# Forgetting attention followed by a gated convolutional FFN on one core: a new order of work, ReLU and weight casts allowed on two engines, the forget gates in one transfer, the last chunk in halves

## The chip, the core and the metric

The kernel runs on one core of a Trainium2 chip. Five engines work side by side, each through its own queue, strictly in the order of that queue: TensorE (PE in the profile, with its weight loads as PEld), VectorE (DVE), ScalarE (ACT), GpSimd (POOL), and SyncE (SP), which does nothing here but issue transfers. An engine whose next instruction waits also holds back everything behind it. Matmuls write PSUM, which this kernel holds as four tiles of 1024 fp32 columns (`ps0` to `ps3`); ACT or DVE has to empty a tile before PE may fill it again. The metric is device microseconds of the whole run; lower is better.

## The reference

Per batch and head (8 x 8, 576 positions of 64 values), causal attention with a decay from the forget gates f, then, on the heads joined to 512 channels, a feed-forward block whose hidden value is gated by a three-tap convolution of itself.

```python
cum = np.cumsum(np.log(np.clip(f, 1e-4, 1.0)), axis=-1)
scores = q @ k.T / 8 + cum[:, :, :, None] - cum[:, :, None, :]   # causal
attn = softmax(scores);  x = (attn @ v) joined to (8, 576, 512)
h = np.maximum(x @ w_in, 0.0)                    # 512 -> 1024
conv = w0 * h[s-1] + w1 * h[s] + w2 * h[s+1]     # along the sequence, per channel
out = (h * sigmoid(conv)) @ w_out                # 1024 -> 512
```

## The kernel before, in words

The program is a list of named tasks (class `Plan`). `ORDER` is the sequence in which the tasks are recorded, and so the sequence in which each engine's queue is filled; `name@ENGINE` chooses the engine where a task may run on more than one. Tiles that are reused (PSUM, score buffers, output buffers) are handed out in that sequence too. Nothing is rescheduled afterwards.

Work goes by half batch (hb 0 to 15: four heads, one PSUM-sized group each) and by batch (b 0 to 7). For half batch `hb` with its two head pairs `i = 2hb` and `2hb+1`:

- `q{hb}.0`, `q{hb}.1`: SP brings q and k from memory with a transposing DMA (`load_qk`, L230), for hb 0 and 1 by plain loads `ld`, PE transposes `tp` and an adjusting copy `cl` (`turned_qk`). The result lies in one of four `qk` tiles (hb modulo 4).
- The decay enters the scores as two more rows of the contraction. hb 1 to 7 get them by `cl` (DVE, L236) and `rw` (L252, L253: rows from the DRAM tensor `image`), hb 8 to 15 by `fi` (`fill`, L244 blanks and L246 rows of `image`), which may go only when both transposes of its half batch have landed. `ki` (POOL) writes `image`; hb 0 adds the decay with extra matmuls.
- `sd`, `so`, `st`: scores on PE (diagonal, off-diagonal, last 64 rows). `ed`, `eo`, `et`: their exponentials on ACT (L401, L418, L380), out of PSUM. `md`, `mt`: causal masks on POOL for hb 8 and later.
- `v{b}.x`: loads of v; `va`: casts of v to fp16; `pv`: attn @ v on PE (L442, L446); `n`: division by the row sum on DVE (L454, L456); `t` and `tx`: transposes on PE and their copies, two of them by DMA (hb 14 and 15).

For batch `b` and hidden chunk `ff` (0 to 7): `f` is x @ w_in (8 matmuls, L482), `r` the ReLU out of PSUM into the fp16 tile `ht` (L492), `c` and `d` the convolution on DVE into `u` (L497, L499), `a` a tanh on ACT (L502), `g` the gate on DVE (L506). The sigmoid is written as half of 1 + tanh, so the ReLU carries a factor of 0.5. `o{b}.{c}` is the product with w_out for 128 rows (L517), `k` copies the last 64 rows aside so that two batches share one matmul group, `e` empties PSUM into an output buffer `ob` (three of them; L523, for the last batch L527), `s` stores it. The weights come by `wi` and `wo` into the same `ob` buffers, and `wic` and `woc` cast them to fp16 (L560).

At the start ACT's queue issues two loads of f (rows 0 to 63 and 64 to 127 of one tile, the same data), loads the table for the logarithm, issues the convolution weights, and takes the logarithm (`dcl`, L313), then loads the table for exp (L314); DVE clips (`dca`, L568), scans (`dcs`) and forms the decay rows (`dck`).

Of the kernel before, what the change touches and what calls it, by code (L numbers as in the profile page):

```python
# [22 lines left out]
n1.0 n1.1 so5.0 t1 q5.0 tx0@DVE eo5.0 tx1@ACT cl3.0 ed5 f0.0 cl5.0 so4.0 r0.0 st2 wi2 c0.0 d0.0 so4.1 f0.1 et2 eo4.1
r0.1 c0.1 d0.1 q5.1 f0.2 v1.0 v1.1 rw3 h0 wic3@POOL eo4.0 v1.4 v1.3 a0.0 wic2@POOL f0.3 r0.2 f0.4 so5.1 a0.1 cl5.1
g0.0 r0.4 c0.4 f0.5 v1.2 rw5 g0.1 r0.3 eo5.1 sd6 r0.5 f0.6 d0.4 a0.4 c0.3 wo2 so6.1 r0.6 q4.1 eo6.1 c0.5 c0.6 st3 et3
sd7 wo1 va2.0@DVE d0.6 so6.0 ed6 pv2.0 sd10 ed7 g0.4 n2.0 va2.1@DVE d0.5 q4.0 c0.2 wo0 va3.0@ACT q6.0 eo6.0 woc2@POOL
f0.7 r0.7 pv2.1 so7.0 v4.0 n2.1 so7.1 ed10 eo7.0 eo7.1 so10.1 d0.3 d0.2 va3.1@POOL cl4.1 st5 eo10.1 sd11 cl4.0 pv3.0
pv3.1 ed11 et5 so11.0 a0.5 a0.2 n3.0 n3.1 woc0@POOL t2 t3 a0.6 rw4 tx2@DVE tx3@DVE so11.1 so10.0 wo3 eo11.0 c0.7 d0.7
q6.1 a0.3 v2.0 v2.4 g0.3 eo10.0 v2.3 woc1@POOL eo11.1 g0.5 f1.0 r1.0 f1.1 f1.2 g0.6 g0.2 f1.3 f1.4 a0.7 v2.2 r1.2 v2.1
g0.7 r1.3 r1.1 c1.0 woc3@ACT c1.2 sd9 st4 va4.0@POOL et4 r1.4 sd8 ed8 d1.0 h1 so9.1 o0.0 ed9 so8.1 cl6.0 cl6.1 so9.0  # L30
o0.1 c1.3 c1.4 va4.1@POOL d1.3 a1.0 g1.0 eo9.1 d1.4 eo9.0 so8.0 f1.5 eo8.1 d1.2 eo8.0 r1.5 rw6 sd12 q7.1 st6 pv4.0
va5.0@POOL va5.1@ACT et6 q7.0 e0.0@DVE c1.1 pv4.1 n4.0 a1.2 k0@DVE a1.4 n4.1 g1.4 ed12 a1.3 q9.1 sd13 zc g1.3 f1.6
ed13 r1.6 t4 tx4@ACT cl7.0 so12.1 eo12.1 pv5.0 pv5.1 c1.6 f1.7 n5.0 n5.1 so12.0 g1.2 r1.7 cl7.1 eo12.0 d1.1 so13.1
c1.7 d1.6 v3.0 v3.4 so13.0 v3.3 rw7 t5 eo13.1 c1.5 d1.5 eo13.0 tx5@ACT v3.2 q9.0 o0.2 v3.1 a1.6 a1.1 o0.3 f2.0 g1.1
e0.1@ACT f2.1 r2.0 a1.5 r2.1 d1.7 c2.0 g1.6 f2.2 st7 v4.2 g1.5 c2.1 et7 a1.7 f2.3 r2.2 fi9 r2.3 sd15 ed15 so15.0 f2.4
eo15.0 d2.0 so15.1 h2 g1.7 sd14 eo15.1 a2.0 ed14 c2.2 d2.2 c2.3 r2.4 d2.1 va7.0@DVE o1.0 c2.4 so14.0 so14.1 eo14.0
eo14.1 va6.0@POOL va6.1@POOL pv6.0 sd18 o1.1 q8.1 ed18 k1@DVE f2.5 d2.4 sd19 a2.4 n6.0 so19.0 g2.4 va7.1@POOL s0.1
e1.0@ACT d2.3 r2.5 pv7.0 ed19 pv7.1 eo19.0 q8.0 st9 et9 v4.3 c2.5 v4.4 n7.0 n7.1 g2.0 v5.0 f2.6 v4.1 md18 a2.2 so19.1
a2.1 fi8 pv6.1 eo19.1 d2.5 f2.7 so18.0 q10.0 md19 r2.6 g2.1 n6.1 s1.0 g2.2 a2.5 r2.7 o1.2 eo18.0 a2.3 t6 c2.6 t7 c2.7
tx6@ACT va8.0@POOL so18.1 tx7@DVE o1.3 f3.0 d2.7 eo18.1 d2.6 f3.1 g2.3 a2.7 va8.1@POOL e1.1@ACT r3.0 sd17 so17.1 g2.5  # L40
g2.7 a2.6 g2.6 r3.1 ed17 c3.0 d3.0 q10.1 f3.2 r3.2 c3.1 f3.3 eo17.1 c3.2 va9.0@DVE r3.3 c3.3 mt9 md17 sd16 ed16 v5.2
o1.4 so16.0 h3 eo16.0 so17.0 d3.2 v5.4 d3.1 d3.3 e1.2@ACT o2.0 fi10 pv9.0 n9.0 k2@DVE st8 q11.0 eo17.0 a3.0 et8 o2.1
a3.1 g3.1 a3.2 sd21 f3.4 va9.1@DVE g3.2 v5.3 s1.2 q11.1 ed21 a3.3 r3.4 e2.0@ACT pv9.1 n9.1 c3.4 f3.5 f3.6 g3.0 r3.5
st10 mt8 d3.4 md16 r3.6 c3.6 so16.1 eo16.1 s1.1 f3.7 so21.0 md21 et10 mt10 sd20 d3.6 o2.2 v5.1 r3.7 eo21.0 c3.7 g3.3
o2.3 a3.4 fi11 q12.0 ed20 a3.6 pv8.0 q12.1 sd23 v6.0 c3.5 st11 e2.1@ACT md20 s2.1 d3.7 a3.7 et11 g3.4 n8.0 va10.0@POOL
pv8.1 n8.1 sd22 so20.0 ed23 d3.5 ed22 t8 tx8@DVE eo20.0 md22 t9 so20.1 tx9@DVE a3.5 va11.0@DVE q13.1 so22.0 eo20.1
g3.6 so22.1 eo22.0 fi12 f4.0 f4.1 r4.0 g3.7 c4.0 d4.0 eo22.1 g3.5 q13.0 mt11 f4.2 r4.1 f4.3 so23.0 so21.1 r4.2 h4
eo23.0 r4.3 a4.0 f4.4 c4.2 d4.2 r4.4 md23 so23.1 v6.2 eo21.1 c4.3 o3.0 o3.1 va10.1@POOL sd25 c4.1 d4.3 a4.2 eo23.1
e3.0@ACT sd24 pv10.0 d4.1 ed24 md24 ed25 fi13 so25.1 c4.4 va11.1@ACT d4.4 q14.1 g4.0 pv10.1 n10.0 a4.3 n10.1 eo25.1
pv11.0 g4.2 a4.1 st12 et12 f4.5 r4.5 mt12 pv11.1 g4.3 f4.6 st13 n11.0 sd26 n11.1 t10 a4.4 g4.4 r4.6 c4.6 et13 ed26  # L50
s3.0 so24.0 c4.5 d4.5 f4.7 d4.6 k3@DVE md25 q14.0 eo24.0 v6.4 o3.2 t11 s2.0 o3.3 tx10@ACT a4.5 r4.7 g4.5 v6.1 sd27
a4.6 c4.7 so26.0 tx11@ACT ed27 v6.3 g4.6 e3.1@ACT s3.1 md26 g4.1 v7.0 d4.7 f5.0 f5.1 r5.0 r5.1 so27.1 eo27.1 c5.0
eo26.0 f5.2 c5.1 d5.1 so25.0 eo25.0 mt13 r5.2 o3.4 md27 so24.1 e3.2@DVE c5.2 d5.2 a4.7 f5.3 va12.0@POOL eo24.1 d5.0
g4.7 r5.3 so26.1 eo26.1 c5.3 so27.0 h5 a5.1 f5.4 f5.5 g5.1 a5.0 va12.1@POOL g5.0 eo27.0 r5.5 d5.3 fi14 o4.0 r5.4 c5.5
sd29 ed29 pv12.0 d5.5 q15.1 n12.0 a5.3 f5.6 va13.0@ACT s3.2 c5.4 st14 v7.4 et14 g5.3 va13.1@DVE v7.1 a5.5 r5.6 o4.1
f5.7 sd28 e4.0@ACT md29 pv13.0 r5.7 c5.6 so28.0 q15.0 ed28 g5.5 v7.3 d5.6 eo28.0 pv12.1 o4.2 c5.7 d5.7 a5.6 n12.1 v7.2
t12 pv13.1 n13.0 d5.4 g5.6 a5.7 a5.2 k4@POOL so29.1 n13.1 g5.7 tx12@ACT o4.3 eo29.1 fi15 a5.4 e4.1@ACT va15.0@POOL t13
s4.1 tx13@DVE sd30 sd31 va14.0@DVE so30.0 f6.0 ed30 md28 va14.1@POOL so29.0 eo30.0 g5.2 r6.0 f6.1 f6.2 va15.1@POOL
eo29.0 c6.0 r6.1 ed31 f6.3 st15 g5.4 d6.0 h6 c6.1 md30 r6.2 r6.3 so28.1 so30.1 et15 c6.2 eo28.1 eo30.1 so31.1 s0.0
c6.3 f6.4 mt15 eo31.1 d6.3 d6.2 pv14.0 mt14 md31 r6.4 n14.0 a6.2 pv14.1 n14.1 k5@DVE g6.2 c6.4 so31.0 eo31.0 f6.5 f6.6  # L60
f6.7 a6.3 r6.6 a6.0 g6.3 c6.6 r6.7 d6.1 pv15.0 d6.6 pv15.1 n15.0 n15.1 a6.6 tx14 tx15 g6.0 a6.1 c6.7 r6.5 o5.0 o5.1
o5.2 c6.5 o5.3 d6.5 a6.5 d6.7 f7.0 f7.1 d6.4 e5.0@ACT g6.6 a6.7 g6.1 a6.4 g6.5 f7.2 g6.4 r7.0 c7.0 g6.7 r7.1 c7.1 f7.3
f7.4 r7.3 e5.1@ACT r7.2 d7.0 f7.5 h7 d7.1 a7.0 a7.1 r7.5 c7.2 o6.0 g7.0 o6.1 o7.0.0 r7.4 g7.1 d7.2 c7.4 o7.1.0 o7.2.0
k6@ACT c7.3 o7.0.1 o7.3.0 c7.5 s5.0 d7.3 o7.2.1 a7.2 g7.2 o7.1.1 d7.4 f7.6 k7.1@DVE e6.0@ACT r7.6 c7.6 o5.4 s6.0
e5.2@ACT o7.2.2 o7.0.2 s5.1 f7.7 a7.3 r7.7 d7.5 a7.5 g7.3 c7.7 o7.3.1 k7.2@DVE o7.3.2 o6.2 d7.7 s5.2 o7.2.3 o7.0.3
a7.4 o7.1.2 o6.3 a7.7 d7.6 g7.4 g7.5 o7.2.4 o7.2.5 o7.1.3 a7.6 o7.1.4 o7.1.5 g7.6 o7.0.4 g7.7 e6.1@ACT k7.3@ACT
k7.5@DVE o7.0.5 o7.0.6 o7.0.7 e7.0@ACT o7.1.6 k7.6@DVE s4.0 s6.1 k7.0@POOL o7.2.6 o7.2.7 k7.4@ACT o7.1.7 e7.1@DVE
# [40 lines left out]
def kernel(  # L108
# [164 lines left out]
    nc.scalar.dma_start(fsb[BH:128], f.rearrange("b h s -> (b h) s"))
# [217 lines left out]
    def relu(b, ff):  # L491
        nc.scalar.activation(ht_of(b, ff)[:, 1:1 + S], ps_of(f"f{b}.{ff}")[:, 0:S], AF.Relu, scale=0.5)  # L492
# [31 lines left out]

    def evac_chunk(b, c, e):
        o, i = ob_t[slot[f"e{b}.{c & ~1}", "ob"]][:, c % 2, :], ps_of(f"o{b}.{c & ~1}.0")[:, 512 * (c % 2):512 * (c % 2 + 1)]
        (nc.scalar.copy if e == "ACT" else nc.vector.tensor_copy)(o, i)  # L527
# [209 lines left out]
```

## Time and profile before

| | us |
|---|---|
| median of 3 runs (lowest, highest) | 255.62 (255.13, 256.41) |
| the profiled execution, whole | 255.41 |
| its span on the core | 253.6 |
| around the span | 1.8 |
| PE, DVE, ACT busy | 231.1, 213.5, 211.4 |
| POOL busy | 62.0 |

The profile is of one execution. Its rows give start and length of an instruction, the line of the kernel that issued it, the tiles that it writes and reads, and in square brackets how long the engine had been idle and which work ended the wait. A queue named SPq or ACTq shows that engine issuing a transfer. The chain that ended last is followed back from the last instruction, each step to what released it.

### The profile page before, as it was taken

The page shows a single profiled execution, that of the slowest core. Times are in us where ns is not written, and L with a number is a line of the kernel's source. Part 1 is how long each engine was busy: PE and PEld are TensorE (multiplying, and loading weights), DVE is VectorE, ACT ScalarE, POOL GpSimd, SP SyncE. Part 2 cuts the span into 40 slices and gives each one's busy share as a digit, 9 for nine tenths or more (in the row PEclk, how much of TensorE's full clock was granted, in tenths as well). Part 3 has the DMA queues.
Part 4 walks back from the last instruction along what each step waited for, and adds up shares of the span by engine and source line. Part 5 has one row for each costly group of instructions (what it writes and reads, how often), then busy time and mean ns, then how long its engine had stood idle before and what let it go on. Part 6 is the DMA issues. An engine that isn't in the chain of part 4 may idle for free.

```text
span 253.6 us, 6451 instructions
## 1 busy us (share of the span) xinstructions
PE 231.1 (91%) x2654; PEld 147.4 (58%) x2654; DVE 213.5 (84%) x329; ACT 211.4 (83%) x283; POOL 62.0 (24%) x91
## 2 busy tenths in 40 slices
...
GB/s 185 320 229 165 222 209 256 215 246 195 236 197 195 215 181 214 216 227 224 217 225 205 187 239 193 197 210 264 230 213 231 87 87 50 24 108 3 277 132 170
DMA packets 116278, 48.81 MB, mean 192 GB/s; under 512 B 106274, under 2 KB 106274, under 8 KB 116248
## 3 DMA queue, kind: packets, MB, share of 16 engines
...
q10 hardware_dynamic: 246, 0.44, 0.6%
...
## 4 chain that ended last, share of the span: by engine, by line
PE 44%; DMA 19%; DVE 13%; ACT 11%; SPq 8%; issue 4%; ACTq 0%; DVEq 0%
PE ps L517 15%; PE ps L482 13%; PE ps L360 8%; DMA qk<-in_q_dram 8%; SPq L230 5%; DVE u L497 3%; PE ps L442 3%; DMA qk<-in_k_dram 3%; ACT pp L418 3%; DVE hg L506 2%; DVE xm L456 2%; DVE u L499 2%; ACT ht L492 2%; ACT hg L502 2%; DMA qk<-image 2%
## 5 line engine op out<-in xcount | busy, mean ns | idle before, releaser
L482 PE MATMUL ps<-xt,w_in_f 128*128 128x512 f16 (+1 forms) x512 | 69.5, 286 | 2.0 <-ACT xt L473 1.1
L418 ACT ACTIVATE pp<-ps 128x1024 f16<-128x1024 f32 x64 | 64.8, 1058 | 6.3 <-PE ps L360 3.4
L360 PE MATMUL ps<-qk 128*128 128x128 bf16 (+2 forms) x576 | 64.4, 243 | 4.2 <-DMA qk<-image 2.9
L517 PE MATMUL ps<-w_out_f,hg 128*128 128x512 f16 x256 | 59.0, 379 | 0.7 <-ACT ob L527 0.7
L499 DVE SCALAR_TENSOR_TENSOR u<-ht,cwt,u 128x576 f32<-128x576 f16 x64 | 55.1, 878 | 0.7
L497 DVE SCALAR_TENSOR_TENSOR u<-ht,cwt 128x576 f32<-128x576 f16 x64 | 53.7, 854 | 2.2 <-ACT ht L492 2.1
L502 ACT ACTIVATE hg<-u,cw 128x576 f16<-128x576 f32 x64 | 49.0, 792 | 6.2 <-DVE u L499 6.0
L360 PEld LDWEIGHTS <-qk 128*128 128x128 bf16 x576 | 40.1, 99 | 23.4 <-issue 6.7
L482 PEld LDWEIGHTS <-w_in_f 128*128 128x128 f16 x512 | 34.2, 98 | 31.1 <-issue 2.3
L506 DVE SCALAR_TENSOR_TENSOR hg<-hg,ht 128x576 f16<-128x576 f16 x64 | 49.6, 799 | 0.4 <-ACT hg L502 0.3
L492 ACT ACTIVATE ht<-ps 128x576 f16<-128x576 f32 x64 | 41.6, 671 | 5.7 <-PE ps L482 3.3
L517 PEld LDWEIGHTS <-hg 128*128 128x128 f16 x256 | 24.1, 98 | 27.4 <-issue 1.0
L404 POOL TENSOR_SCALAR_AFFINE_SELECT pp<-pd 128x1024 f16<-128x1024 f32 x16 | 20.4, 1275 | 46.6 <-ACT pd L401 46.6
L456 DVE TENSOR_TENSOR xm<-ps,rc 128x896 f16<-128x896 f32 (+1 forms) x32 | 24.3, 758 | 1.1
L442 PE MATMUL ps<-va,pp 128*128 128x65 f16 x640 | 24.3, 193 | 0.1
L442 PEld LDWEIGHTS <-pp 128*128 128x128 f16 x640 | 22.4, 98 | 2.0 <-DVE va L267 0.2
L267 POOL CAST va<-vf 128x1024 f16<-128x1024 f32 x8 | 10.1, 1265 | 49.0 <-DMA vf<-in_v_dram 25.1
L401 ACT ACTIVATE pd<-ps 128x1024 f32<-128x1024 f32 x16 | 16.6, 1045 | 2.3 <-PE ps L360 2.2
L454 DVE RECIPROCAL rc<-ps 128x14 f32<-128x14 f32 (+1 forms) x32 | 6.6, 206 | 13.6 <-PE ps L442 9.6
L401 ACT ACTIVATE pp<-ps 128x1024 f16<-128x1024 f32 x16 | 16.5, 1059 | 0.0
L368 PE MATMUL ps<-mask,ident 128*128 128x512 bf16 (+1 forms) x40 | 14.3, 358 | 2.3 <-ACT ht L492 1.5
L523 ACT COPY ob<-ps 128x1024 f32<-128x1024 f32 (+1 forms) x15 | 14.4, 958 | 2.3 <-DMA out_dram<-ob 1.1
...
## 6 DMA issues: line engine op xcount, KB each, us to landing
...
```

What stands on the lines that cost most here:

```text
L360: nc.tensor.matmul(o, tk[:, h * S + k0:h * S + k0 + 128], tq[:, h * S + q0:h * S + q0 + n], start=first, stop=last and not by_matmul(hb, h))
L401: nc.scalar.activation(o, ps_of(f"sd{i}").rearrange("p (s c) -> p s c", s=2), AF.Exp, scale=SCALE)
L418: nc.scalar.activation(pair(i)[:, s, 512:1536], ps_of(f"so{i}.{s}"), AF.Exp, scale=SCALE)
L442: nc.tensor.matmul(ps[:, c:c + D + 1], block(hb, h, m, n), va[:, h, m, 0:D + 1], start=(m == 0), stop=(m == n))
L456: nc.vector.tensor_tensor(x.rearrange("p (j h d) -> p j h d", j=a, d=D), got[:, :, :, 0:D], r.unsqueeze(3).broadcast_to((128, a, g, D)), o ...
L482: nc.tensor.matmul(ps[:, c:c + n], w_in_f16[:, cc, 128 * ff:128 * (ff + 1)], xt[:, cc // 2, x:x + n], start=(cc == 0), stop=(cc == NCC - 1))
L492: nc.scalar.activation(ht_of(b, ff)[:, 1:1 + S], ps_of(f"f{b}.{ff}")[:, 0:S], AF.Relu, scale=0.5)
L497: nc.vector.scalar_tensor_tensor(u, ht[:, 0:S], cwt[:, ff, 0:1], ht[:, 1:1 + S], op0=ALU.mult, op1=ALU.add)
L499: nc.vector.scalar_tensor_tensor(u, ht[:, 2:2 + S], cwt[:, ff, 1:2], u, op0=ALU.mult, op1=ALU.add)
L502: nc.scalar.activation(hg_of(b, ff), u_t[slot[f"c{b}.{ff}", "u"]], AF.Tanh, scale=cw[:, ff, 1:2])
L506: nc.vector.scalar_tensor_tensor(hv, hv, 1.0, ht_of(b, ff)[:, 1:1 + S], op0=ALU.add, op1=ALU.mult)
L517: nc.tensor.matmul(ps[:, 512 * (c % 2):512 * (c % 2 + 1)], w, w_out_f16[:, ff, :], start=(ff == 0), stop=(ff == NFF - 1))
```

## The change

The forget gates are loaded by one transfer that repeats the 64 rows, instead of two. The loading of the exp table becomes a task of its own, `tb`, after `dcl`. The ReLU may run on ACT or on DVE (there as multiply by 0.5, then maximum with 0), and the weight casts on POOL, ACT or DVE. The second 128-row chunk of the last batch (`e7.1`, `s7.1`) is emptied in two halves of 256 columns, one by ACT and one by DVE, and stored in two halves, one issued by SP and one by ACT. `ORDER` is written anew throughout. By the new table eight of the 64 ReLUs run on DVE (r0.1, r0.6, r1.5, r1.7, r2.1, r3.0, r4.0, r4.2); two of the four casts of w_in move from POOL to ACT; of w_out, DVE has three and POOL one, where POOL had three and ACT one. DVE loses three of five casts of v (`va`, the large part), four of five `k` copies and one emptying copy, and has nine copies `tx` instead of seven, of them tx0 and tx1.

```diff
-ld0 ld0.0.0 dca cw dcl ld0.1.0 ld0.0.1 ld0.1.1 cwt tp0.0.0 tp0.0.1 tp0.1.0 ld1 ld1.0.0 ld1.0.1 dcs tp0.1.1 cl0.0.0@ACT
...
+ld0 ld0.0.0 dca dcl tb ld0.0.1 cw cwt tp0.0.0 ld0.1.0 ld0.1.1 ld1 ld1.0.0 ld1.0.1 tp0.0.1 tp0.1.0 v0.0 v0.1 q2.0 q2.1
...
-    nc.scalar.dma_start(fsb[0:BH], f.rearrange("b h s -> (b h) s"))
-    nc.scalar.dma_start(fsb[BH:128], f.rearrange("b h s -> (b h) s"))
+    nc.scalar.dma_start(fsb, f.rearrange("b h s -> (b h) s").unsqueeze(0).broadcast_to((2, BH, S)))
...
     def decay_log():
         nc.scalar.activation(fsb, fsb, AF.Ln)
-        nc.scalar.preload_act_table(AF.Exp)
...
-    def relu(b, ff):
-        nc.scalar.activation(ht_of(b, ff)[:, 1:1 + S], ps_of(f"f{b}.{ff}")[:, 0:S], AF.Relu, scale=0.5)
+    def relu(b, ff, e):
+        o, i = ht_of(b, ff)[:, 1:1 + S], ps_of(f"f{b}.{ff}")[:, 0:S]
+        if e == "ACT":
+            nc.scalar.activation(o, i, AF.Relu, scale=0.5)
+        else:
+            nc.vector.tensor_scalar(o, i, 0.5, 0.0, op0=ALU.mult, op1=ALU.max)
...
+    def evac_half(b, c, x):
+        o = ob_t[slot[f"e{b}.{c & ~1}", "ob"]][:, c % 2, 256 * x:256 * (x + 1)]
+        i = ps_of(f"o{b}.{c & ~1}.0")[:, 512 * (c % 2) + 256 * x:512 * (c % 2) + 256 * (x + 1)]
+        (nc.vector.tensor_copy if x else nc.scalar.copy)(o, i)
+
+    def store_half(b, c, x):
+        r = b * S + 128 * c
+        (nc.scalar if x else nc.sync).dma_start(outf[r:r + 128, 256 * x:256 * (x + 1)],
+                                                ob_t[slot[f"e{b}.{c & ~1}", "ob"]][:, c % 2, 256 * x:256 * (x + 1)])
...
+    add("tb", "ACT", [], lambda: nc.scalar.preload_act_table(AF.Exp), behind=["dcl"])
...
-            add(f"{w}c{j}", "POOL/ACT", [f"{w}{j}"], lambda e, w=w, j=j: stage_cast(w, j, e), give=[("ob", f"{w}{j}")])
+            add(f"{w}c{j}", "POOL/ACT/DVE", [f"{w}{j}"], lambda e, w=w, j=j: stage_cast(w, j, e), give=[("ob", f"{w}{j}")])
...
-            add(f"r{b}.{ff}", "ACT", [f"f{b}.{ff}"], lambda b=b, ff=ff: relu(b, ff), take=["ht"], give=[("ps", f"f{b}.{ff}")])
+            add(f"r{b}.{ff}", "ACT/DVE", [f"f{b}.{ff}"], lambda e, b=b, ff=ff: relu(b, ff, e), take=["ht"], give=[("ps", f"f{b}.{ff}")])
...
+                if c == 1:
+                    for x in range(2):
+                        add(f"e{b}.{c}.{x}", ("ACT", "DVE")[x], [f"o{b}.{c}.{NFF - 1}"], lambda b=b, c=c, x=x: evac_half(b, c, x),
+                            behind=[f"e{b}.{c - 1}"])
+                        add(f"s{b}.{c}.{x}", ("SP", "ACT")[x], [f"e{b}.{c}.{x}"], lambda b=b, c=c, x=x: store_half(b, c, x))
+                    continue
```

Three places show how the queues move. The first is SP's queue from the plain loads of hb 1 to the transposes of hb 2 and the rows of hb 1 and 2 (`hg1` holds the plain loads, `vf0` the first batch of v, `qk2` and `qk1` the tiles of hb 2 and hb 1). Before:

```order
L209 DMA hg1_129<-in_k_dram 128x2x576
L230 DMA_TRANSPOSE qk2_87<-in_k_dram 128x2304
L230 DMA_TRANSPOSE qk2_87<-in_q_dram 128x2304
L259 DMA vf0_89<-in_v_dram 128x8x64 x3
L259 DMA vf0_89<-in_v_dram 64x8x64
L252 DMA qk1_86<-image_65 1x2304
L253 DMA qk1_86<-image_65 2x2304
```

And now:

```order
L211 DMA hg1_129<-in_k_dram 128x2x576
L261 DMA vf0_89<-in_v_dram 128x8x64 x2
L232 DMA_TRANSPOSE qk2_87<-in_q_dram 128x2304
L232 DMA_TRANSPOSE qk2_87<-in_k_dram 128x2304
L261 DMA vf0_89<-in_v_dram 128x8x64 x2
L254 DMA qk1_86<-image_65 1x2304
L255 DMA qk1_86<-image_65 2x2304
```

Two loads of v moved ahead of the two transposes, and one went behind the rows of hb 1.

The second place is SP's queue from the rows of hb 10 (`qk2`, task fi10) to those of hb 11 (`qk3`, task fi11). Before:

```order
L230 DMA_TRANSPOSE qk2_87<-in_k_dram 128x2304
L259 DMA vf1_90<-in_v_dram 128x8x64
L259 DMA vf1_90<-in_v_dram 64x8x64
L244 DMA qk2_87<-blank_66 60x4x1152
L246 DMA qk2_87<-image_65 4x2x2304
L230 DMA_TRANSPOSE qk3_88<-in_q_dram 128x2304
L259 DMA vf1_90<-in_v_dram 128x8x64
L541 DMA out_0_dram<-ob1_131 64x512 x2
L230 DMA_TRANSPOSE qk3_88<-in_k_dram 128x2304
L538 DMA out_0_dram<-ob2_132 128x2x512
L259 DMA vf1_90<-in_v_dram 128x8x64
L244 DMA qk3_88<-blank_66 60x4x1152
```

And now:

```order
L232 DMA_TRANSPOSE qk2_87<-in_q_dram 128x2304
L552 DMA out_0_dram<-ob0_130 128x2x512
L232 DMA_TRANSPOSE qk3_88<-in_q_dram 128x2304
L246 DMA qk2_87<-blank_66 60x4x1152
L248 DMA qk2_87<-image_65 4x2x2304
L232 DMA_TRANSPOSE qk3_88<-in_k_dram 128x2304
L555 DMA out_0_dram<-ob0_130 64x512 x2
L552 DMA out_0_dram<-ob2_132 128x2x512
L246 DMA qk3_88<-blank_66 60x4x1152
```

The first transpose of hb 11 moved ahead of fi10, the second directly behind it, and the loads of v went out of this stretch.

The third place is the end of ACT's queue, from the last tanh on (`tl` takes the last rows, `ob` the results, L527 before and L531 and L536 after are the emptying copies of the last batch). Before:

```order
L502 ACTIVATE hg1_129<-u3_127,cw_71 128x576
L523 COPY ob0_130<-ps1_134 128x1024
L511 COPY tl1_115<-hg1_129 128x64
L527 COPY ob1_131<-ps2_135 128x512
L511 COPY tl1_115<-hg1_129 128x64
L527 COPY ob0_130<-ps0_133 128x512
L541 DMA out_0_dram<-ob0_130 64x512
L527 COPY ob2_132<-ps3_136 128x512
```

And now:

```order
L527 COPY ob0_130<-ps1_134 128x1024
L506 ACTIVATE hg1_129<-u2_126,cw_71 128x576
L527 COPY ob1_131<-ps2_135 128x512
L506 ACTIVATE hg1_129<-u0_124,cw_71 128x576
L515 COPY tl1_115<-hg1_129 128x64 x3
L531 COPY ob1_131<-ps0_133 128x512
L536 COPY ob1_131<-ps0_133 128x256
L540 DMA out_0_dram<-ob1_131 128x256
L531 COPY ob2_132<-ps1_134 128x512
L555 DMA out_0_dram<-ob2_132 64x512
L531 COPY ob0_130<-ps3_136 128x512
```

The copies e6.1 (1024 columns) and e5.2 (512) now stand ahead of the last tanh; before, e6.1 came behind it. A half copy with its own transfer stands ahead of the last two copies.

111 lines of the change are left out of this document (57 added, 54 removed).

## The prediction

> **What bounds the kernel now.** I read the page first, then stretches of the span, then the chain of waits, then single queues where the chain leaves PE.
>
> ```profile
> span 253.6 us, 6451 instructions
> PE 231.1 (91%) x2654; PEld 147.4 (58%) x2654; DVE 213.5 (84%) x329; ACT 211.4 (83%) x283; POOL 62.0 (24%) x91
> ```
>
> No engine is idle enough to be ignored: three stand at 83 to 91 per cent of the span. So the time is the start, the end, and the holes between; the stretch view (DVE alone) sizes the middle:
>
> ```profile
> core 0: us, DVE busy (x), PEclk, DMA share, GB/s
> 41.05:243.70 202.65, 191.67 (x281) 0.99 0.89 186
> 137.00:148.00 11.00, 7.43 (x11) 0.84 0.98 208
> ```
>
> From its first convolution (41.05) to its last gate (243.70) DVE idles 202.65 - 191.67 = 10.98 us. One stretch of 11 us holds 3.57 of them; the other 7.41 are scattered over 190 us. So from 41 us on the kernel is nearly DVE's own length. What can move is: when 41.05 comes, that one hole, the scattered idle, DVE's load, and the 9.9 us behind its last gate. I cost the change by these five.
>
> **The start.** These rows, from the timeline and (0.80 and 32.53) the chain, show what holds back 41.05.
>
> ```profile
> 0.80 4.29 DMA u<-in_f_dram
> 1.38 0.62 ACTq L273 DMA_DIRECT2D u<-in_f_dram  x1
> 7.34 0.46 DVE L568 TENSOR_SCALAR u<-u 128x576 f32<-128x576 f32 x1 [2.97 <-DMA u<-in_f_dram]
> 5.11 0.37 SPq L209 DMA_DIRECT2D hg<-in_k_dram  x1
> 5.52 5.92 SPq L230 DMA_TRANSPOSE qk<-in_k_dram  x1
> 38.68 0.67 ACT L492 ACTIVATE ht<-ps 128x576 f16<-128x576 f32 x1
> 32.53 7.70 DMA qk<-in_q_dram
> 40.26 0.88 DVE L236 TENSOR_SCALAR qk<-qk,lim 128x2304 uint16<-128x2304 uint16 x1 [3.55 <-DMA qk<-in_q_dram]
> 41.05 0.81 DVE L497 SCALAR_TENSOR_TENSOR u<-ht,cwt 128x576 f32<-128x576 f16 x1
> ```
>
> f lands at 7.34, behind its second transfer. One transfer spares the issue of 0.62 us and can hardly land before 5.09, where the first of the two did. So the logarithm comes 0.6 to 2.2 us sooner. That alone is worth nothing at 41.05: the first ReLU is done at 39.35, and DVE stands at cl5.0 until 40.23, when the transpose of q for hb 5 lands. DVE's order still has cl5.0 ahead of c0.0. SP's set of transfers up to that transpose is the same, so only SP's waits can give time. Before, the long issue 5.52 to 11.44 stands behind the loads of f; now two loads of v, some 0.6 each (half of the pair at 129.95 below), fill that place and are out of the way later. Bounds for c0.0: 0 (the DMA engines carry the same bytes) to -2.2 (all of f's gain passes on). I take -1.2, about the two loads. The task `tb` costs nothing, since it still follows `dcl` directly on ACT. The two casts of w_in on ACT lie ahead of r0.0, and ACT has 0.9 us between 39.35 and 40.23, plus what tx1 leaves by going to DVE.
>
> **The hole.** SP's queue, with what waited:
>
> ```profile
> 123.58 0.89 SPq L244 DMA_DIRECT2D qk<-blank  x1
> 125.27 3.95 SPq L230 DMA_TRANSPOSE qk<-in_q_dram  x1
> 129.95 1.21 SPq L541 DMA_DIRECT2D out_dram<-ob  x2
> 131.20 7.62 DMA qk<-in_k_dram
> 138.84 0.95 SPq L244 DMA_DIRECT2D qk<-blank  x1
> 139.84 4.59 DMA qk<-image
> 144.57 1.22 PE L360 MATMUL ps<-qk 128*128 128x128 bf16 x12 [2.39 <-DMA qk<-image]
> 147.04 0.18 DVE L454 RECIPROCAL rc<-ps 128x4 f32<-128x4 f32 x1 [3.45 <-PE ps L446]
> ```
>
> From fi10 (123.58) to the landed rows of hb 11 (144.43) SP needs 20.9 us: fi10 1.7, one transpose, a load and a store until 131.20, the second transpose landing 7.6 later, then 5.6 for fi11. With the first transpose ahead of fi10 and the second directly behind it, the 5.93 between 125.27 and 131.20 fall out: 14.9. The work that PE has in the meantime, counted in tasks from the order and priced by chain rows:
>
> ```profile
> 116.56 0.44 PE ps L360 x4
> 121.57 1.96 PE ps L482 x16
> 126.57 1.73 PE ps L517 x8
> 128.30 1.00 PE ps L442 x32
> 111.62 0.25 PE ps L442 x8
> 109.39 0.44 PE ps L446 x20
> ```
>
> Before, from fi10 to sd23: 4 `f` (0.98), 3 `o` (1.73), two large `pv` (1.00), one small (0.69), four score groups (0.44) and two tails (0.11), 13.8 us. Now, from fi10 to st11: 6 `f`, 3 `o`, two large `pv`, two small, six score groups and a tail, 17.2. Cover rises from 7 us under the need (of which PE's other delays hid all but 2.39) to 2.3 above it. I take the whole hole, -3.5 (DVE's 3.45). Bounds: 0, if SP comes to fi10 some 5.8 late, and -3.57.
>
> **DVE's load.** Prices from the groups by shape:
>
> ```profile
> L267 DVE CAST va<-vf 128x1024 f16<-128x1024 f32 x5 | 3.6, 718 | 0.0
> L473 DVE COPY xt<-ps 128x1152 f16<-128x1152 f16 x7 | 5.1, 751 | 0.6 <-PE ps L465 0.5
> L511 DVE COPY tl<-hg 128x512 f16<-128x512 f16 x5 | 2.0, 403 | 0.0
> L527 DVE COPY ob<-ps 128x512 f32<-128x512 f32 x2 | 1.3, 685 | 2.3 <-issue 2.3
> ```
>
> No ReLU ran on DVE. Its 576 fp32 columns out of PSUM lie between the 512-column copy (0.685) and that times 576/512 (0.77); I take 0.75. Behind 41.05: eight ReLUs +6.0, three weight casts +2.15 (the shape of the first row), one `tx` more +0.75, three casts of v fewer -2.15, four `k` fewer -1.6, one 512-column copy fewer -0.7: +4.45. ACT sheds 8 x 0.67 = 5.4 of ReLU for them, but gets casts and copies; I give that no credit. What of the 4.45 shows? It can go into 7.41 us of scattered idle. Bounds 0 and +4.45; I take half, +2.2, since neither end has a row for it.
>
> POOL matters for DVE too. These two rows overlap; the same instruction later, alone, is the third:
>
> ```profile
> 41.66 1.10 POOL L560 CAST w_in_f<-ob 128x1024 f16<-128x1024 f32 x1 [3.79 <-DMA ob<-in_moe_w_in_dram]
> 41.97 1.40 DVE L499 SCALAR_TENSOR_TENSOR u<-ht,cwt,u 128x576 f32<-128x576 f16 x1
> 44.21 0.82 DVE L499 SCALAR_TENSOR_TENSOR u<-ht,cwt,u 128x576 f32<-128x576 f16 x1
> ```
>
> A POOL cast beside DVE cost DVE 0.58 us. Behind 41.05 POOL now does two weight casts and two small casts of v less, one large cast of v and two `k` more: one instruction fewer, which I count as nothing. The Trainium skill (SBUF — State Buffer, "SBUF: two separate sides") has it that a DVE instruction with two SBUF inputs and a GpSimd instruction that reads SBUF take turns on a shared port, the later one waiting for all of the other. The trace agrees in kind, at 0.58 of 1.10 us here. By that rule a cast gone from POOL would return up to its whole length, and for the one instruction fewer the sum would be about 1.1 us lower than mine.
>
> **The end.** From the chain, and the last two tanh on ACT:
>
> ```profile
> 240.30 1.50 ACT L502 ACTIVATE hg<-u,cw 128x576 f16<-128x576 f32 x2 [0.42 <-DVE u L499]
> 243.48 4.50 DMA out_dram<-ob
> 248.07 0.59 ACT ob L527
> 248.69 0.55 ACTq L541
> 249.35 0.59 ACT ob L527
> ```
>
> e7.4 stands until the store of e6.1 has left its buffer, then ACT issues for 0.55, copies e7.3, and the last store takes 3.65 to 253.6. The last tanh begins near 241.05: 12.55 us to the end. Now e6.1 and e5.2 go before the last tanh, but e7.0 writes e5.2's buffer. Let T be the last tanh's start, which is e5.2's end: 1.2 for its two issues (129.95 above), some 3.6 to land, like the last store, then on ACT e7.0 0.59, half copy some 0.4, issue 0.55, e7.4 0.59, issue 0.55, e7.3 0.59, small gaps 0.2, store 3.65: T + 11.9. That is -0.6. Splitting e7.1 itself shortens nothing: its half issue on ACT (0.55) is in front of the two last copies. Bounds: +0.5 (that issue on the path, no wait saved) to -1.4 (no buffer wait).
>
> **Sum.** The profiled execution took 255.41, 1.8 outside its span and 0.21 under the median 255.62. -1.2 - 3.5 + 2.2 - 0.6 = -3.1: **252.3 us**.
>
> **Rivals.** *The load eats the gain* (no change): if all 4.45 shows and the start gives nothing, 255.41 - 3.5 + 4.45 - 0.6 = 255.8. For it: DVE is over 95 per cent busy outside the hole. Against: the new load is small beside 7.41 of idle.
>
> *ReLU at the head of DVE's queue* (slower): a DVE ReLU waits for its `f` on PE, and every convolution, gate and norm behind it waits too. If PE only begins that `f` when DVE arrives, each costs 0.98. In the order r3.0 has one DVE instruction between its `f` and itself, r4.2 two, the others more; PE would have to run late as it did at 144.57. All eight at full price give 252.3 + 7.8 = 260.1; from five on (257.2) it ends slower by over half a per cent, and I price it at six, 258.2.
>
> *More of the scattered idle closes* (faster still): DVE's whole new load hides and 2 us of the 7.41 go as well: 255.41 - 1.2 - 3.5 - 2.0 - 0.6 = 248.1. For it: ACT, which DVE waits for in places, loses 5.4 of ReLU. Against: no single place in the rows shows it.
>
> **Chances.** My forecast 0.48, the load eats the gain 0.12, ReLU at the head or the like 0.25, more closes 0.15. Half a per cent, about what a measurement of this kernel tells from no change, is 254.3 to 256.9: faster 0.63, same 0.12, slower 0.25. The range goes from a little under the third rival, 247.0, to a little over the second, 258.5; my own case alone spans 250.0 to 254.3.
>
> **What would show it.** c0.0 on DVE near 39.9 with cl5.0 still ahead of it; no wait of PE for rows of `image` over 0.5 us; DVE's idle between its first convolution and last gate under 8 us; some 0.75 for a ReLU on DVE; about 12 us from the last tanh to the end. I am wrong if PE waits for `image` or a transpose elsewhere, if DVE idles before its ReLUs, or if c0.0 comes later than 41.

## The result, and the profile after

The changed kernel takes 264.08 us (median of 4 runs, 263.23 to 264.54), against 256.01 for the kernel before (median of 4 runs, three of them those of the table above): 1.032 times as long, 95% interval [1.028, 1.037]. Slower, then, and outside the range given. Ratios here and below are of undisturbed runs alone; since single runs of one kernel spread by 3 per cent and more, the medians of all runs stand beside a ratio that is near 1.

The profiled execution of the changed kernel took 264.21, with these totals and these stretches (DVE alone):

```profile
span 262.5 us, 6468 instructions
PE 230.8 (88%) x2654; PEld 146.8 (56%) x2654; DVE 216.8 (83%) x331; ACT 213.2 (81%) x286; POOL 57.7 (22%) x87
```

```profile
core 0: us, DVE busy (x), PEclk, DMA share, GB/s
51.48:253.19 201.71, 195.76 (x280) 1.00 0.89 186
10.00:11.00 1.00, 0.00 (x0) 1.00 0.46 161
12.00:13.00 1.00, 0.00 (x0) 1.00 0.13 51
14.00:15.00 1.00, 0.00 (x0) 1.00 0.13 50
```

The first row is the stretch from the first convolution to the last gate. It takes 201.71 where before it took 202.6, with 5.95 of DVE idle where there were 10.98. So the middle is a little shorter. The loss lies ahead of it: the first convolution begins at 51.48, not at 41.05.

The last rows say where that comes from. From about 11 to 15 us DVE does nothing and the 16 DMA engines together are 0.13 to 0.16 busy, which is about two engines' worth (2/16 = 0.125), moving 48 to 58 GB/s. Before, the microseconds from 10 to 15 had a share of 0.95 to 1.55; the middle one of them:

```profile
12.00:13.00 1.00, 0.97 (x2) 1.00 1.19 266
```

The timeline of the changed kernel shows what everybody stands for:

```profile
0.81 1.17 ACTq L274 DMA_DIRECT2D u<-in_f_dram  x1
2.05 0.31 ACTq L276 DMA_DIRECT2D pd<-in_moe_conv_w_dram  x1
15.19 0.46 DVE L582 TENSOR_SCALAR u<-u 128x576 f32<-128x576 f32 x1 [10.82 <-DMA u<-in_f_dram]
15.68 0.68 ACT L314 ACTIVATE u<-u 128x576 f32<-128x576 f32 x1 [12.39 <-DVE u L582]
3.22 0.47 SPq L211 DMA_DIRECT2D hg<-in_k_dram  x1
15.18 0.99 SPq L261 DMA_DIRECT2D vf<-in_v_dram  x2
42.55 4.48 SPq L232 DMA_TRANSPOSE qk<-in_q_dram  x1
50.69 0.88 DVE L238 TENSOR_SCALAR qk<-qk,lim 128x2304 uint16<-128x2304 uint16 x1 [2.44 <-DMA qk<-in_q_dram]
51.48 0.81 DVE L501 SCALAR_TENSOR_TENSOR u<-ht,cwt 128x576 f32<-128x576 f16 x1
52.21 0.76 DVE L496 TENSOR_SCALAR ht<-ps 128x576 f16<-128x576 f32 x1
```

and the waits of its first 20 us (what waited, for what, us in all, times, longest):

```profile
PE ps L342 <- DMA pd<-in_moe_conv_w_dram: 15.6, 1, 15.6
ACT u L314 <- DVE u L582: 12.4, 1, 12.4
DVE u L582 <- DMA u<-in_f_dram: 10.8, 1, 10.8
```

f lands at 15.19, where before its second transfer had landed at 7.34. DVE stands for it 10.8 us and ACT behind DVE 12.4. PE stands 15.6, for the convolution weights, which were issued behind f on the same queue and land only with it. SP stands from 3.7 to 15.18; the profile names the landing of f as what ended it. All four queues shift together, and the transpose of q for hb 5, on which the first convolution's predecessor `cl5.0` waits, is asked for at 42.55 instead of 32.53.

The hole is gone. SP's queue there, and the longest waits of PE between 52 and 242 us, of the changed kernel:

```profile
130.99 3.17 SPq L232 DMA_TRANSPOSE qk<-in_q_dram  x1
134.27 0.91 SPq L246 DMA_DIRECT2D qk<-blank  x1
135.93 4.60 SPq L232 DMA_TRANSPOSE qk<-in_k_dram  x1
142.56 0.93 SPq L246 DMA_DIRECT2D qk<-blank  x1
```

```profile
PE ps L442 <- DVE ht L496: 1.8, 1, 1.8
PE ps L482 <- ACT pp L418: 1.7, 2, 1.6
PE ps L360 <- DVE xm L456: 0.8, 1, 0.8
```

No row of `image` is among them. The longest wait is now for a ReLU on DVE (L496) that had not yet emptied its PSUM tile: 1.8 us, once.

The end, from the chain of the changed kernel:

```profile
244.29 10.81 PE ps L521 x50
255.16 0.59 ACT ob L531
255.75 0.28 ACT ob L536
256.06 0.43 DVE ob L536
256.51 0.39 ACTq L540
257.00 0.59 ACT ob L531
257.62 0.56 ACTq L555
258.22 0.59 ACT ob L531
```

The two halves of e7.1 did not run side by side: DVE's half begins when ACT's is done, and ACT issues the half store only behind it, so that ACT's next copy begins at 257.00, 0.97 after its half (256.03).

From the last gate's end to the end of the span it takes 262.5 - 253.19 = 9.31, before 253.6 - 243.67 = 9.93. The account closes: +10.43 at the first convolution, -0.91 behind it, -0.62 at the end, +8.9 of span.

### The profile page after: what moved, and what is told of

The parts are those of the page before. It is cut to its first block, busy times and chain, and to the rows that moved or that the text cites. A ratio compares the mean times of both kernels' runs of the same rounds, so it can differ in the third digit from the quotient of the medians.

```text
span 262.5 us, 6468 instructions
## 1 busy us (share of the span) xinstructions
PE 230.8 (88%) x2654; PEld 146.8 (56%) x2654; DVE 216.8 (83%) x331; ACT 213.2 (81%) x286; POOL 57.7 (22%) x87
## 4 chain that ended last, share of the span: by engine, by line
PE 49%; DVE 23%; DMA 10%; ACT 6%; issue 4%; SPq 4%; ACTq 1%; POOL 1%; DVEq 0%
PE ps L521 16%; PE ps L482 14%; PE ps L360 7%; DVE u L501 6%; DVE u L503 6%; DMA pd<-in_moe_conv_w_dram 5%; PE ps L442 4%; ACT pp L418 3%; DVE hg L510 3%; DMA qk<-in_k_dram 3%; DVE xm L456 2%; SPq L232 2%; PE ps L218 2%; DMA ob<-in_moe_w_out_dram 2%; PE ps L463 1%
## 5 line engine op out<-in xcount | busy, mean ns | idle before, releaser
L503 DVE SCALAR_TENSOR_TENSOR u<-ht,cwt,u 128x576 f32<-128x576 f16 x64 | 57.8, 916 | 1.3 <-DVE u L501 0.5
L360 PEld LDWEIGHTS <-qk 128*128 128x128 bf16 x576 | 39.4, 98 | 21.1 <-issue 5.2
L510 DVE SCALAR_TENSOR_TENSOR hg<-hg,ht 128x576 f16<-128x576 f16 x64 | 47.8, 767 | 0.3 <-ACT hg L506 0.2
L494 ACT ACTIVATE ht<-ps 128x576 f16<-128x576 f32 x56 | 36.2, 663 | 4.2 <-PE ps L482 2.4
L404 POOL TENSOR_SCALAR_AFFINE_SELECT pp<-pd 128x1024 f16<-128x1024 f32 x16 | 19.5, 1225 | 58.0 <-ACT pd L401 58.0
L269 POOL CAST va<-vf 128x1024 f16<-128x1024 f32 x9 | 11.9, 1328 | 36.5 <-PE ps L360 13.3
L527 ACT COPY ob<-ps 128x1024 f32<-128x1024 f32 (+1 forms) x16 | 15.1, 947 | 4.2 <-PE ps L521 2.9
L342 PE MATMUL ps<-one,pd 3*128 3x3 f32 x8 | 1.0, 241 | 15.6 <-DMA pd<-in_moe_conv_w_dram 15.6
```

The source lines that it names most:

```text
L360: nc.tensor.matmul(o, tk[:, h * S + k0:h * S + k0 + 128], tq[:, h * S + q0:h * S + q0 + n], start=first, stop=last and not by_matmul(hb, h))
L494: nc.scalar.activation(o, i, AF.Relu, scale=0.5)
L503: nc.vector.scalar_tensor_tensor(u, ht[:, 2:2 + S], cwt[:, ff, 1:2], u, op0=ALU.mult, op1=ALU.add)
L510: nc.vector.scalar_tensor_tensor(hv, hv, 1.0, ht_of(b, ff)[:, 1:1 + S], op0=ALU.add, op1=ALU.mult)
```

## The experiments

Theory A: the one transfer of f does it, and why it is slow is the count of its outermost dimension. Its rivals: the new order's own start (B), the reading of the same rows twice (C), one large transfer as such (D).

### f in two transfers again; the kernel before with f in one

```diff
 # e1_two_f: the changed kernel
-    nc.scalar.dma_start(fsb, f.rearrange("b h s -> (b h) s").unsqueeze(0).broadcast_to((2, BH, S)))
+    nc.scalar.dma_start(fsb[0:BH], f.rearrange("b h s -> (b h) s"))
+    nc.scalar.dma_start(fsb[BH:128], f.rearrange("b h s -> (b h) s"))
 # e2_before_one_f: the kernel before, the other way round
```

> The changed kernel with the gates loaded by two transfers again, everything else as changed. Theory A (the one transfer of f is carried by 2 of the 16 DMA engines, since its outer dimension counts 2, and the whole loss is its late landing): f lands near 7 us instead of 15.2, the first convolution starts near 41 us instead of 51.5, and the whole takes 264.1 less 8 to 10.4, so 253.7 to 256. Theory B (the new order of the start, with two loads of v ahead of the transposes, is what came late): f may land early, but the first convolution stays later than 46 us and the whole above 259.

> The kernel before with only the one transfer of f put in. Theory A: f lands near 15 us instead of 7.3, and the whole takes 8 to 10.5 us more than before, 264 to 266.5. Theory B: the old order hides it, and the whole stays within 2 us of before, 254 to 258.

Measured: with two transfers the changed kernel takes 255.16 (12 runs; before 254.95), ratio 0.998 [0.993, 1.003]. With one transfer the kernel before takes 261.06, ratio 1.025 [1.019, 1.032]. So the one line carries the whole loss of the changed kernel, and it costs the kernel before 2.5 per cent by itself. The timeline of `e1_two_f`:

```profile
7.30 0.46 DVE L583 TENSOR_SCALAR u<-u 128x576 f32<-128x576 f32 x1 [2.94 <-DMA u<-in_f_dram]
43.84 0.88 DVE L238 TENSOR_SCALAR qk<-qk,lim 128x2304 uint16<-128x2304 uint16 x1 [1.92 <-DMA qk<-in_q_dram]
44.63 0.81 DVE L502 SCALAR_TENSOR_TENSOR u<-ht,cwt 128x576 f32<-128x576 f16 x1
```

and of `e2_before_one_f`:

```profile
15.22 0.46 DVE L567 TENSOR_SCALAR u<-u 128x576 f32<-128x576 f32 x1 [10.86 <-DMA u<-in_f_dram]
```

f lands at 7.30 and 15.22: the form of the transfer decides, whichever order stands around it. But both expectations missed in part. In `e1_two_f` the first convolution comes at 44.63, not near 41: it stays short of the 46 that theory B asked for, but the new start is late by itself, by 3.6 us here. Two more runs below with the same order up to there, `e6_relu_act` and `e8_hole_back`, have it at 44.62 and 43.33, so single traces of one order differ by 1.3 us at this place. The waits of SP in its first 46 us name a copy of hb 1 that the rows of `image` for hb 1 stand for, with the transposes queued behind them:

```profile
SPq L254 <- DVE qk L226: 2.4, 1, 2.4
```

And `e2_before_one_f`, for which 264 to 266.5 was expected, took 261.06: its first convolution comes 9.1 us late (50.13), but 3.2 of this are won back behind it (199.42 from the first convolution to the last gate's end, 202.62 before). By their size these 3.2 are the hole. PE's waits for `image`, in the kernel before and in `e2_before_one_f`, are

```profile
PE ps L360 <- DMA qk<-image: 2.9, 2, 2.4
```

```profile
PE ps L359 <- DMA qk<-image: 0.2, 1, 0.2
```

SP's order is the old one in both, and the wait of 2.39 is gone all the same in a run that is some 9 us late. What in the delay closes it is open; so the order on SP is not the only thing that decides about this wait.

### The outermost count of the transfer

Rows of v stand in for the gates, which are left out; the clip from 0.9 keeps the numbers tame. 128 rows of 576 values are read in 2, 4 or 16 groups that lie apart.

```diff
 # e3_v2; e3_v4: [64 * S, 4], [S, 32]; e3_v16: 16 groups of 8
-    nc.scalar.dma_start(fsb, f.rearrange("b h s -> (b h) s").unsqueeze(0).broadcast_to((2, BH, S)))
+    nc.scalar.dma_start(fsb, bass.AP(tensor=v.tensor, offset=int(v.offset), ap=[[128 * S, 2], [S, 64], [1, S]]))
-    ... 1e-4, 1.0, op0=ALU.max, op1=ALU.min
+    ... 0.9, 1.0, op0=ALU.max, op1=ALU.min
```

> The changed kernel, with the 128 rows of the gate tile read from v instead of f, in one transfer of 2 groups of 64 rows that lie apart, so nothing is repeated; the clip starts at 0.9 so that all values are alike. The gates are thus left out of the result; the bytes and the instructions stay. Theory A (2 groups, 2 DMA engines): it lands at 14 to 16 us as f did, with a DMA share near 0.13 while it is alone. Rival C (reading the same rows of f twice is what is slow): it lands by 9 us.

> As e3_v2 and e3_v16: 128 rows of the tensor v, clipped from 0.9, stand in for the gates (the gates are left out), in one transfer of 4 groups of 32 rows. Theory A (the outermost count of the transfer decides how many DMA engines work): twice the two engines of e3_v2, the rows land between 8 and 10 us, and the first convolution comes at 43.5 to 47. Rival C' (a few groups are slow for another reason, or any count over two is spread): 15 or 5.3 us.

> The same with one transfer of 16 groups of 8 rows that lie apart. Theory A (16 groups, 16 engines): it lands by 9 us, and the first convolution starts before 43 us. Rival C, and rival D (one transfer of 288 KB behind the loads of q and k is slow whatever its form): it lands as in the run with 2 groups; for D that is 14 to 16 us.

The clip of `e3_v2`, of `e3_v4` and of `e3_v16` (one run each):

```profile
15.25 0.46 DVE L582 TENSOR_SCALAR u<-u 128x576 f32<-128x576 f32 x1 [10.88 <-DMA u<-in_v_dram]
```

```profile
10.86 0.46 DVE L582 TENSOR_SCALAR u<-u 128x576 f32<-128x576 f32 x1 [6.49 <-DMA u<-in_v_dram]
```

```profile
5.28 0.49 DVE L582 TENSOR_SCALAR u<-u 128x576 f32<-128x576 f32 x1 [0.91 <-DMA u<-in_v_dram]
```

| groups | rows landed, us | first convolution, us | whole time, us |
|---|---|---|---|
| 2 | 15.25 | 52.24 | 263.62 |
| 4 | 10.86 | 47.66 | 259.87 |
| 16 | 5.28 | 43.63 | 257.33 |

Each row of the table moves as many bytes from the same tensor by one instruction. Two groups of rows that are read once are as slow as the broadcast of the same 64 (C falls), and one transfer of 16 groups lands earlier than the two transfers did (D falls). So the time falls as the outermost count grows. Only with two groups is the transfer seen alone, from 12 to 15 us at a share of 0.12 to 0.13; with four, other loads are under way until it lands (0.94 from 10 to 10.6 us), so that four working engines are argued, not seen. Two expectations were missed by a little: the rows of `e3_v4` came 0.9 us later than the window given and its first convolution 0.7, and the first convolution of `e3_v16` came at 43.63, not before 43.

### What the late f holds up

```diff
+    nc.scalar.dma_start(cwrow, moe_conv_w)
     nc.scalar.dma_start(fsb, f.rearrange("b h s -> (b h) s").unsqueeze(0).broadcast_to((2, BH, S)))
     nc.scalar.preload_act_table(AF.Ln)
-    nc.scalar.dma_start(cwrow, moe_conv_w)
```

> The changed kernel, f in its one transfer, but the convolution weights issued ahead of it on ACT's queue. It tells what the late f holds up. If most of the 10.4 us is the queue (the convolution weights behind f, and with them PE's first transposes): PE starts at 4 to 8 instead of 15.6 and the first convolution comes at 44 to 47. If it is f itself (the decay rows that hb 0 and 1 need, and SP, which stands for f): PE starts early, f still lands at 15.2, and the first convolution stays at 49 to 52.

The timeline of `e10_cw_first`:

```profile
4.42 1.01 PE L342 MATMUL ps<-one,pd 3*128 3x3 f32 x8 [4.42 <-DVE one L298]
5.37 2.10 PE L218 MATMUL ps<-ident_b,hg 128*128 128x128 bf16 x18
16.64 1.12 PE L218 MATMUL ps<-ident_b,hg 128*128 128x128 bf16 x9 [7.64 <-DVE cw L345]
```

PE now starts at 4.4, and stops again at 9.0 for 7.6 us: the copy that frees its PSUM tile (L345) stands on DVE behind the clip, which stands for f until 16.03. So the queue behind f was one of several chains to the same transfer, and taking it away alone gives nothing. The second case was right in kind, but not for SP: here SP goes on at 3.94 with its loads of v, though f is under way until 16.03. So SP's stand in the changed kernel was not a need for f itself, and what it was stays open.

The size was not right either: the first convolution comes at 55.06 and the run takes 272.15 (one run), 3.6 us later than in the changed kernel at the first convolution and 4.4 us longer behind it (206.07). The trace shows where the 3.6 arise: the score products of hb 0 take PE 5.50 us (from 21.09 to 26.59), in the changed kernel 3.05 (from 20.36 to 23.41), so the copy of hb 1 begins at 27.37 instead of 24.19, and SP, which stands for it 5.6 us there, stands 10.1 here. Why PE is slower at these products no run shows, nor where the 4.4 come from.

### The late start of the new order

`e4_old_start` has f in two transfers, the order of the kernel before up to `c0.0`, and the new order for everything else. `e9_start_relu` has, beyond that, the eight ReLUs of DVE on ACT, and `e11_cl5_later` also `cl5.0` behind `d0.1` instead of ahead of `c0.0`.

```diff
 # e4_old_start
-ld0 ld0.0.0 dca dcl tb ld0.0.1 cw cwt tp0.0.0 ld0.1.0 ...
+ld0 ld0.0.0 dca cw dcl tb ld0.1.0 ld0.0.1 ld0.1.1 cwt tp0.0.0 ...
 # e9_start_relu, on top
-r0.1@DVE ... r0.6@DVE ... r4.2@DVE
+r0.1@ACT ... r0.6@ACT ... r4.2@ACT
 # e11_cl5_later, on top
-cl5.0 ... c0.0 ... d0.0 ... c0.1 ... d0.1
+c0.0 ... d0.0 ... c0.1 ... d0.1 cl5.0
```

> The changed kernel with f in two transfers, and its order of work replaced, up to the first convolution (c0.0), by that of the kernel before; from c0.0 on the new order. Theory B (beside the transfer of f, the new order's own start is late: PE takes the scores of hb 0 between the transposes of hb 1, SP stands 2.4 us for the copy of hb 1, and so q of hb 5 is asked for at 36.05 instead of 32.53): c0.0 comes back to about 41, the stretch from the first convolution to the last gate stays at 201 to 202 and the end at 9.3, so 41.05 + 201.5 + 9.3 + 1.8 = 253.7 against the 255.4 of the profile before, a ratio of 0.991 to 0.996. Rival (the late start is taken up behind c0.0, where PE and ACT pace the work): c0.0 at about 41, but the stretch behind it as much longer, and the ratio stays at the 0.998 of e1_two_f.

> As e4_old_start (f in two transfers, order of the kernel before up to the first convolution, new order behind it), and the eight ReLUs of DVE on ACT. If what the single traces show adds up (c0.0 at 41.65 in e4_old_start, 199.6 from the first convolution to the last gate in e6_relu_act, 8.8 to 9.3 at the end): span 250.1 to 252, ratio 0.985 to 0.994, the first version that beats both kernels. Rival (what is won at the start is lost behind it, as 1.2 us were in e4_old_start): the stretch takes 201 to 203 and the ratio is 0.995 to 1.003.

> As e9_start_relu, and on DVE the decay copy of hb 5 (cl5.0, which stood 2.81 us for the transpose of q in e4_old_start) moved behind the first two convolutions. If that wait is what holds the first convolution: c0.0 at 40.2 to 40.8, when the first ReLU is done, and the ratio 0.003 to 0.006 under that of e9_start_relu. Rival (the scattered waits of DVE behind c0.0 take it back): the stretch as much longer, the same ratio as e9_start_relu.

| | first convolution | from there to the last gate's end | span | median (before) | ratio |
|---|---|---|---|---|---|
| e1_two_f | 44.63 | 201.73 | 255.3 | 255.16 (254.95) | 0.998 [0.993, 1.003] |
| e4_old_start | 41.65 | 202.94 | 253.4 | 256.04 (256.01) | 0.998 [0.990, 1.007] |
| e9_start_relu | 41.04 | 202.80 | 252.7 | 255.10 (255.48) | 1.011 [1.006, 1.016] |
| e11_cl5_later | 40.34 | 205.93 | 255.2 | 254.83 (255.48) | 1.002 [0.998, 1.006] |

The first convolution goes where it was expected, 3 to 4 us earlier. The time doesn't follow: none of the three is faster than the kernel before by more than the noise, and behind the earlier start the stretch is longer in these single traces. `e4_old_start` has 1.2 us more than `e1_two_f`. The two with the ReLUs on ACT are to be held against `e6_relu_act` below (199.58), and have 3.2 and 6.4 more; in `e11_cl5_later` 0.9 of it is `cl5.0` itself, now inside the stretch, and its trace is of a run of 256.90, 2.1 above its median. So the rivals were right in kind, as far as the runs can tell: the medians agree with those of the kernel before within 0.3 per cent. The ratio of `e9_start_relu`, 1.011, lies outside both of its cases. It is not to be read closely: the ratios of `e9_start_relu` and `e11_cl5_later` differ by 0.9 per cent, their medians, beside the same runs of the kernel before, by 0.1. No version of this study beats the kernel before by more than the noise.

### The load on DVE

The same edit as in `e9_start_relu`, but with the new order's own start.

```diff
-r0.1@DVE ... r0.6@DVE ... r4.2@DVE
+r0.1@ACT ... r0.6@ACT ... r4.2@ACT
```

> The changed kernel with f in two transfers and the eight ReLUs of DVE on ACT, at the same places of the order. The prediction's step (DVE is the bound, half of a load added to it shows): 6.0 us less on DVE shortens the stretch from the first convolution to the last gate by about 3, ratio to before 0.985 to 0.990. Rival (ACT, which then gets 5.3 more, holds DVE up in these places, so that the ReLUs on DVE cost nothing): 0.997 to 1.01, DVE idle in that stretch 9 to 13 instead of 6 to 7 us.

The stretch from the first convolution to the last gate's end in `e6_relu_act`, and in `e1_two_f`:

```profile
core 0: us, PE busy (x) PEld busy (x) DVE busy (x) ACT busy (x) POOL busy (x), PEclk, DMA share, GB/s
44.62:244.20 199.58, 193.15 (x2205) 119.00 (x2205) 189.81 (x272) 184.12 (x258) 50.28 (x51) 1.00 0.91 189
```

```profile
44.63:246.36 201.73, 194.08 (x2213) 119.65 (x2211) 195.19 (x280) 181.21 (x251) 49.22 (x51) 1.00 0.89 187
```

From the same start, 5.4 us less on DVE shorten the stretch by 2.15, two fifths of it. (The trace of `e1_two_f` is of a run of 257.05, 1.9 above its median, that of `e6_relu_act` of 254.79, 0.1 above, so part of the 2.15 can be the difference of two runs.) DVE's idle rises from 6.5 to 9.8 us and ACT gets 2.9 more. In the ratio it doesn't show, as the rival had it: 1.002 [0.998, 1.006], median 254.70 (before 256.01). And with the start of before (`e9_start_relu` against `e4_old_start`) the same edit gives 0.1 us of stretch. Between none and two fifths of such a load is on the path. Two traces don't settle it closer.

### The hole, both ways

`e8_hole_back` is the changed kernel with f in two transfers and the transposes of hb 11 put back. `e12_before_hole` is the kernel before with nothing but those two moved forward.

```diff
 # e8_hole_back (the order from q11.0 on, tasks of SP alone)
-q11.0 fi10 q11.1 s1.2 s1.0 fi11
+fi10 q11.0 s1.2 q11.1 s1.0 fi11
 # e12_before_hole
-fi10 q11.0 v5.3 s1.2 q11.1 s1.1 v5.1 fi11
+q11.0 fi10 q11.1 v5.3 s1.2 s1.1 v5.1 fi11
```

> The changed kernel with f in two transfers, and on SP's queue the two transposes of hb 11 put back behind the rows of hb 10 (fi10), the second behind the store of two 64-row pieces, as before. The prediction's step (the hole was this order on SP): from fi10 to the landed rows of hb 11 SP needs some 20.7 us again against 17.2 of PE's work, PE waits 2 to 3.5 us for rows of image, and the ratio is 0.998 + 2.4/255 to 0.998 + 3.5/255 = 1.007 to 1.012. Rival (the hole went because the loads of v left that stretch, or because PE comes later anyway): no wait over 1 us, ratio 0.995 to 1.001.

> The kernel before, with one thing of the new order: on SP's queue the first transpose of hb 11 ahead of the rows of hb 10 (fi10), the second directly behind them. The prediction's step alone: PE's wait of 2.39 and DVE's of 3.45 for the rows of hb 11 go, the stretch from the first convolution to the last gate falls from 202.6 to 199 to 200.2, ratio 0.986 to 0.991. Rival (fi10 now comes 4 us later, and PE waits for the rows of hb 10 instead): a wait for image of 1 to 3 us near 128 to 136, the stretch 201.5 to 203, ratio 0.995 to 1.002.

The row of PE that waits in `e8_hole_back`:

```profile
143.85 0.28 PE L361 MATMUL ps<-qk 128*128 128x64 bf16 x4 [2.54 <-DMA qk<-image]
```

The wait comes back with the order on SP, at the place and of the size of before (2.39 there); `e1_two_f` has none there. The ratio is 1.013 [1.005, 1.020] where `e1_two_f` had 0.998; the medians are 258.17 (4 runs) and 256.01, 0.8 per cent apart. The stretch shows less of it: 202.61 against 201.73. So with f early and the new order around it, SP's order does set this wait. But the reverse isn't a gain by itself. The timeline of `e12_before_hole`:

```profile
134.57 1.22 SPq L541 DMA_DIRECT2D out_dram<-ob  x2
135.84 0.59 SPq L538 DMA_DIRECT2D out_dram<-ob  x1
139.08 1.01 ACT L523 COPY ob<-ps 128x1024 f32<-128x1024 f32 x1 [1.93 <-DMA out_dram<-ob]
140.15 0.71 PE L360 MATMUL ps<-qk 128*128 128x64 bf16 x8 [1.57 <-ACT ob L523]
141.23 0.82 DVE L497 SCALAR_TENSOR_TENSOR u<-ht,cwt 128x576 f32<-128x576 f16 x1 [1.83 <-ACT ht L492]
```

PE waits for `image` 0.5 us at most. But the transposes that went forward push three stores back by 4.6 and 0.65 us (before they were issued at 129.95 and 135.19), so ACT waits 1.93 for an output buffer, PE 1.57 for ACT and DVE 1.83 for a ReLU behind that copy. Stretch 203.23, ratio 1.006 [1.000, 1.011] (medians 256.53 and 255.48): the rival's number, by another wait than the rival named. From 130 to 150 us DVE idles 4.26, against 4.42 in the same 20 us behind the first convolution before (129.4 to 149.4), so the move is an even exchange in these two traces; that the stretch is 0.6 longer fits a wait ahead of the moved transfers: PE stands 2.6 us at 45 us for a cast of w_in on POOL (0.2 before). In the new order the loads of v had left this place and the stores fall into it later, and the hole closes there without this: in `e1_two_f` ACT waits for no output buffer between 120 and 165 us.

## Why the prediction was wrong

**The step that failed** is the first term of the sum: "One transfer spares the issue of 0.62 us and can hardly land before 5.09 ... So the logarithm comes 0.6 to 2.2 us sooner", with "Bounds for c0.0: 0 (the DMA engines carry the same bytes) to -2.2". The DMA engines carried the same bytes, but two of them did it. f came 7.85 us later, and the first convolution 10.43 later where -1.2 stood in the sum. The price of a transfer was taken from its bytes and its issue, and the bound from above was set at 0 with no reason from a row against a loss. The rows of before have transfers of few outermost rows (those of `image`, 2x2304), but small ones, and the prediction priced none of them. This is the whole of the slowdown: with that line undone the same kernel is at 0.998 of before. It is most of the miss, but not all: 0.988 was forecast (252.3 over 255.41), so about one per cent is gain that did not come.

The Trainium skill has the rule that was missed (DMA: Bandwidth & Descriptors, "Rules for kernel authors"): a leading broadcast of c copies confines a transfer to at most c engines; "Why a DMA increments its semaphore by 16 and not by 1" says how the number is chosen, the largest up to 16 that divides the slowest dimension of both sides. The trace agrees: share 0.13 at two, and the rows landed at 15.25, 10.86 and 5.28 us with 2, 4 and 16. The same table of the Trainium skill advises one transfer of 128 partitions rather than two of disjoint halves; for a source of this form the measurement says the opposite, 7.3 with two and 15.2 with one.

**c0.0 for its other reason.** The prediction had the new order bring the first convolution forward, since two loads of v fill SP's long issue. Without the slow transfer it came 2.3 to 3.6 us later in three traces, and with the start of before it went back to 41.65. SP stood 2.4 us of this for a copy of hb 1, and PE now takes scores of hb 0 between the transposes of hb 1; the prediction looked only at which transfers stand ahead on SP, not at what each of them waits for. It was also wrong that such a shift passes on: 3 to 4 us at c0.0 changed no time that could be measured.

**The hole, -3.5.** The mechanism was right in part. With f in two transfers PE has no wait at this place (two of 0.41 and 0.57 for other rows of `image`, at 46 and 68 us), and 2.54 again when SP's order is put back. But the order is not the only thing that closes it: `e2_before_one_f` closed it with the old order, in a run some 9 us late. The changed kernel has both the new order and the delay, so there the closing can't be put down to the order alone. The size isn't settled either: putting the wait back cost 0.9 us of stretch between two single traces and 1.4 per cent (3.7 us) between two ratios whose intervals nearly touch, while the medians lie 0.8 per cent (`e8_hole_back`) and 0.1 per cent (`e1_two_f`) over those of before. In the kernel before, the same move only exchanges it for a wait for output buffers. Together the two terms of the middle, -3.5 and +2.2, were to give -1.3; measured, -0.91. That these lie so near is luck in part: by DVE's own rows it is 4.12 more work and 5.03 less idle, not half of the load and the hole alone.

**DVE's load, +4.45, half of it on the path.** DVE's work in the stretch grew by 4.1 (195.76 against 191.64), a ReLU there takes 0.75 (as given). None to two fifths of such a load showed when it was taken away. No run separates the term for POOL, which was counted as nothing.

**The end, -0.6.** From the last tanh, as the prediction counted, it takes 11.3 us (251.22 to 262.5), not 11.9: -1.3 against the 12.55 of before, twice the term. That it is -0.62 from the last gate's end is another measure, and the likeness to -0.6 is luck. The mechanism was another too: not a buffer but PE's products (until 255.10 in the chain) set when the last copies begin.

**The rivals.** Of "ReLU at the head of DVE's queue" one case appeared, from the other side: PE waited 1.8 us for a ReLU on DVE. "The load eats the gain" gave no change, which is what `e1_two_f` measured once the transfer was undone, and near its way: the start gave nothing, and DVE's stretch had 3.55 more work for 4.44 less idle. "More closes" was not seen in any time. No rival named the transfer, so the range had no room for it. Of what was to prove the forecast wrong, the sentence "if c0.0 comes later than 41" did.

Leaving the first term out, the forecast was 252.3 + 1.2 = 253.5, 0.993 of the profile before (255.41); `e1_two_f` measured 0.998 [0.993, 1.003], so a gain of that size lies at the edge of the interval and is not shown.
